# Half of one weight tile moved onto eight of the sixteen DMA engines, at the end of a decode block's weight stream

## The chip, the cores and the metric

The kernel runs on one core of a Trainium2 chip. The metric is device time in microseconds (us) of one launch. Before the change the median of three runs is 774.22 us (774.18 to 774.46).

## The reference

A decoder block for one token in each of two sequences (B = 2, D = 1024), all in float32: layer norm, cached attention with 32 query heads on 4 key/value heads of 128 over 32768 cached positions, and beside it a dense layer with SiLU; both are added to the input.

```python
xn = _layernorm(x, axis=-1)
return x + _A_ref(xn, A_k_cache, A_v_cache, A_wq, A_wo) + _B_ref(xn, B_w1, B_w2)

# _A_ref: q = x @ wq; softmax(q k^T / sqrt(Dh)) v, then  o.reshape(B, Sq, Hq * Dh) @ wo
# _B_ref: h = silu(x @ w1) with 3584 columns;  out = h @ w2
```

Keys, values and weights are some 331 MB, and each of them is used once.

## The kernel before, in words

SBUF holds three buffers `bufA`, `bufB` and `bufC` of 128 partitions x 16384 floats (8 MB each). Everything large passes through them, by transfers that one queue, SP's, issues in program order (`load`, L203). First come wq and w1 and their matmuls. Then eight loops, one for each pair of key/value head and sequence, take two blocks of keys and two of values, 8 MB each.

The last part is the product with the output weights, cut into 60 row tiles of 128 rows x 1024 columns: 32 of wo, 28 of w2. They add into one result. `plan` (L344) loads wo's first half into bufA, its second into bufC, and the first 16 tiles of w2 into bufB. When TensorE has finished with bufA (`i_wo0`, L376), the last 12 tiles of w2 go there in nine pieces (L377), each with a semaphore of its own (`piece4` to `piece12`): six tiles, two tiles, then three times one tile, then the last tile in four quarters. `stream` (L335) issues the pieces from the list of their cuts; `tiles` (L352) walks over the row tiles and lets TensorE wait for the piece that ends a tile. Row tile 57 is the third last (columns 9 D to 10 D of bufA, the tenth tile there). The quarters of row tile 59 have a loop of their own (L383). The result of tile 59 goes through ScalarE to `ot` (L389) and by a transfer of ScalarE's queue to the output (L390).

A source of 128 rows x n columns moves as 128 packets of n x 4 bytes, one for each partition, shared by 16 DMA engines: eight packets on each. Each engine works through the queue's transfers in their order, and a piece has landed when the last of its engines has signalled.

## Time and profile before

| | |
|---|---|
| median of three runs | 774.22 us |
| the profiled execution: its time | 774.62 us |
| the profiled execution: its span from first to last instruction | 773.1 us |
| TensorE busy with matmuls | 391.9 us, 51% |
| moved from memory | 331 MB, 429 GB/s over the span |
| DMA engines busy | 99.2% on SP's queue |

The profile divides the span into 40 slices and gives for each the busy share of every engine and of the 16 DMA engines. Rows of the trace give an instruction's start from the span's begin, the engine, the program line, and what ended the idle time ahead of it. A share of DMA of 1.00 is all 16 engines busy, 0.50 eight of them.

### The profile page before, as it was taken

What the parts mean: (1) busy time and instruction counts of PE and PEld (TensorE: products, weight loads), DVE (VectorE), ACT (ScalarE), POOL (GpSimd) and SP (SyncE); (2) the same over time, 40 slices, a digit from 0 to 9 for tenths busy, and PEclk for the clock granted to TensorE, in tenths of its full rate; (3) what the DMA queues carried; (4) which work ended last, traced back from release to release, by engine and by line L of the source; (5) the groups of instructions that cost most, each with busy time, mean ns of one, the idle gap of its engine ahead of it and who ended that gap; (6) DMA issues with size and microseconds to landing.
All of it is one profiled execution on the core that took longest, in us unless ns stands there. A gap on an engine that the chain in (4) does not pass through costs nothing. (4 is left out here: it accounts for less than half of the span.)

```text
span 773.1 us, 6135 instructions
## 1 busy us (share of the span) xinstructions
PE 391.9 (51%) x2736; PEld 121.8 (16%) x2736; DVE 130.5 (17%) x241; ACT 30.6 (4%) x49; POOL 3.0 (0%) x10
## 2 busy tenths in 40 slices
PE   1545645454545444545454555454554454555476
PEld 1111211111111111111111111111211121111111
DVE  2000015001410150015001410141014001410000
ACT  0000101000100010001000000000001000000000
POOL 1000000000000000000000000000000000000000
PEclk9977677677677677677677667667767667667679
DMA  9999999999999999999999999999999999999997
GB/s 384 434 435 431 434 435 434 435 434 434 434 434 434 434 434 434 434 434 434 434 434 434 431 434 434 431 434 434 434 434 434 434 434 434 434 434 434 420 427 302
DMA packets 7094, 331.51 MB, mean 429 GB/s; under 512 B 798, under 2 KB 1318, under 8 KB 1708
## 3 DMA queue, kind: packets, MB, share of 16 engines
q1 hardware_dynamic: 7056, 331.35, 99.2%
q8 instruction: 6, 0.10, 0.0%
q10 hardware_dynamic: 28, 0.02, 0.0%
q14 instruction: 4, 0.03, 0.0%
HBM read 331.37 MB, written 0.01 MB: 429 GB/s over the span
## 5 line engine op out<-in xcount | busy, mean ns | idle before, releaser
L97 PE MATMUL ps<-bufB,qT 128*32 128x512 f32 x512 | 73.8, 740 | 82.3 <-PEq L52 82.3
L97 PE MATMUL po<-bufB,st 128*32 128x512 f32 x512 | 72.3, 728 | 80.2 <-PEq L52 80.2
L97 PE MATMUL ps<-bufA,qT 128*32 128x512 f32 x512 | 72.9, 733 | 66.4 <-PEq L52 66.4
L97 PE MATMUL po<-bufA,st 128*32 128x512 f32 x512 | 74.6, 748 | 49.5 <-PEq L52 49.5
L250 DVE STREAM_TRANSPOSE st<-ps 128x512 f32<-128x512 f32 x32 | 22.9, 717 | 245.4 <-PE ps L97 245.4
L97 PEld LDWEIGHTS ps<-bufB,qT 128*32 128x32 f32 x512 | 20.2, 132 | 135.9 <-issue 135.9
L97 PEld LDWEIGHTS po<-bufB,st 128*32 128x32 f32 x512 | 19.9, 131 | 132.6 <-issue 132.6
L286 DVE RECIPROCAL rl<-smA 128x8 f32<-128x8 f32 x8 | 1.7, 208 | 222.7 <-PE smA L97 222.7
L97 PEld LDWEIGHTS ps<-bufA,qT 128*32 128x32 f32 x512 | 20.0, 131 | 112.7 <-issue 112.7
L97 PEld LDWEIGHTS po<-bufA,st 128*32 128x32 f32 x512 | 20.5, 134 | 97.1 <-issue 97.1
L252 DVE TENSOR_REDUCE mx<-st 128x8 f32<-128x512 f32 x32 | 34.8, 1086 | 1.1
L273 ACT ACTIVATE st<-st 128x512 f32<-128x512 f32 x32 | 20.2, 630 | 359.7 <-DVE st L272 358.7
L278 DVE TENSOR_REDUCE ls<-st 128x8 f32<-128x512 f32 x32 | 33.5, 1068 | 0.8
L97 PE MATMUL ps<-bufB,xnT 128*32 128x512 f32 x112 | 18.5, 737 | 14.6 <-PEq L52 14.6
L272 DVE TENSOR_TENSOR st<-st,gmax 128x512 f32<-128x512 f32 x32 | 21.2, 685 | 0.3
L97 PE MATMUL ps<-bufA,xnT 128*32 128x512 f32 x64 | 9.8, 778 | 13.1 <-PEq L52 13.1
L97 PE MATMUL ps<-bufC,oT 128*32 128x512 f32 x64 | 10.0, 790 | 9.9 <-DMA bufC<-in_wo 9.9
L97 PE MATMUL ps<-bufC,xnT 128*32 128x512 f32 x64 | 8.7, 705 | 10.7 <-DMA bufC<-in_w 10.7
L284 ACT COPY ob<-po 128x512 f32<-128x512 f32 x8 | 4.7, 585 | 232.8 <-PE po L97 232.8
L97 PE MATMUL ps<-bufA,oT 128*32 128x512 f32 x64 | 9.4, 750 | 8.6 <-DMA bufA<-in_wo 8.6
L97 PE MATMUL smA<-ident,rm 128*8 128x128 f32 x16 | 3.6, 314 | 18.6 <-PEq L52 18.6
L188 DVE COPY qall<-ps 128x16 f32<-128x16 f32 x4 | 0.5, 170 | 62.1 <-PE ps L97 62.1
(65 smaller groups left out, 109.3 us busy)
## 6 DMA issues: line engine op xcount, KB each, us to landing
bufB<-in_w SPq DMA_DIRECT2D x1, 6144.0 KB, 26.1
bufB<-in_w SPq DMA_DIRECT2D x1, 5632.0 KB, 43.0
bufA<-in_w SPq DMA_DIRECT2D x1, 3072.0 KB, 36.5
bufB<-in_w SPq DMA_DIRECT2D x1, 2560.0 KB, 48.7
bufA<-in_w SPq DMA_DIRECT2D x3, 512.0 KB, 40.3
bufA<-in_w SPq DMA_DIRECT2D x1, 1024.0 KB, 38.7
bufA<-in_w SPq DMA_DIRECT2D x4, 128.0 KB, 38.1
bufA<-in_kt SPq DMA_DIRECT2D x8, 29.2
```

Of the source, the lines that this page charges most:

```text
L97: return nc.tensor.matmul(o, lhsT, rhs, start=start, stop=stop)
L188: m = V.tensor_copy(qall[:, B * h:B * (h + 1), :].rearrange("p b (j i) -> p b j i", j=2), o[:, :, 2 * j:2 * j + 2, :].rearrange("p i j b - ...
L250: t = dve.mark(V.transpose(st[:, a].rearrange("p j m -> p (j m)"), ps[a]))
L252: m = dve.mark(V.tensor_reduce(mx[:, a, :], st[:, a].rearrange("p j (r m) -> p m (j r)", r=4), AX.X, ALU.max))
L272: act.wait(dve.mark(V.tensor_sub(e8, e8, gmax.to_broadcast([P, 64, REP]))))
L273: expd.append(act.mark(nc.scalar.activation(st[:, a], st[:, a], AF.Exp, scale=SCALE)))
L278: t = dve.mark(V.tensor_reduce(ls[:, a - 1, :], e8.rearrange("p n m -> p m n"), AX.X, ALU.add))
L284: act.tell(tob, act.mark(nc.scalar.copy(ob, po)))
L286: t = dve.mark(V.reciprocal(rl, smA[:, :REP]))
```

## The change

The list of cuts gets one more entry, so that row tile 57 comes in two transfers of half a tile's width (512 columns) each. The first half is an ordinary piece. The second half does not come from `w2` but from a new input `w2h`, which the host fills with the same numbers laid out as 16 x 8 x 512: element (r, e) is the row of partition 16 e + r. The transfer reads it with the axis e outermost, as 8 x 16 rows of 512 floats. TensorE waits for both halves ahead of tile 57, and the quarters' semaphores move on by one place.

```diff
-    pieces = []
+    pieces, w2h = [], w2h.rearrange("r e n -> e r n")
...
             s = sem(f"piece{len(pieces)}")
-            load(buf[:, lo:hi], src[:, lo:hi], s, *ticks)
+            if buf is bufA and src is not wo[0] and hi == 10 * D:
+                load(buf[:, lo:hi], w2h, s, *ticks)
+            else:
+                load(buf[:, lo:hi], src[:, lo:hi], s, *ticks)
...
-            pe.wait((next(s for hi, s in ends if hi >= (i + 1) * D), 16))
+            pe.wait(*((s, 16) for hi, s in ends if i * D < hi < (i + 1) * D),
+                    (next(s for hi, s in ends if hi >= (i + 1) * D), 16))
...
-    ends = [*stream(bufA, w2[:, W:], (0, 6 * D, 8 * D, 9 * D, 10 * D, lo, lo + QW, lo + 2 * QW, lo + 3 * QW,
+    ends = [*stream(bufA, w2[:, W:], (0, 6 * D, 8 * D, 9 * D, 9 * D + D // 2, 10 * D, lo, lo + QW, lo + 2 * QW, lo + 3 * QW,
                                       lo + D), i_wo0)]
...
-        pe.wait((ends[5 + u][1], 16))
+        pe.wait((ends[6 + u][1], 16))
...
+    half = arrays["w2"][:, (FT - 3) * D + D // 2:(FT - 2) * D]
+    arrays["w2h"] = lay(half, (8, 16, D // 2), (1, 0, 2), (16, 8, D // 2))
```

On SP's queue, at its end, where the pieces of w2 for bufA are issued (`in_w` is w2, `in_w2h` the new input):

```order
 L206 DMA bufA<-in_w 128x2048 [waits pe]
-L206 DMA bufA<-in_w 128x1024 [waits pe] x3
+L206 DMA bufA<-in_w 128x1024 [waits pe]
+L206 DMA bufA<-in_w 128x512 [waits pe]
+L206 DMA bufA<-in_w2h 128x1x512 [waits pe]
+L206 DMA bufA<-in_w 128x1024 [waits pe]
 L206 DMA bufA<-in_w 128x256 [waits pe] x4
```

The queue issues ten transfers there instead of nine; the four quarters stay last.

On TensorE, at row tiles 56 to 58 (`acc` is the result's bank; piece numbers count the transfers of this part):

```order
 L97 MATMUL acc<-bufA,hT 32x256 [waits piece6]
 L97 MATMUL acc<-bufA,hT 32x256 x3
-L97 MATMUL acc<-bufA,hT 32x256 [waits piece7]
+L97 MATMUL acc<-bufA,hT 32x256 [waits piece8,piece7]
 L97 MATMUL acc<-bufA,hT 32x256 x3
-L97 MATMUL acc<-ob,fold 32x256 [waits dve,piece8]
+L97 MATMUL acc<-ob,fold 32x256 [waits dve,piece9]
```

The matmuls and their order are the same; tile 57 waits for two semaphores instead of one.

## Rows read from the trace of the kernel before

**Rows 1.** The profile page: its slices and its DMA queues.
```profile
DMA  9999999999999999999999999999999999999997
GB/s 384 434 435 431 434 435 434 435 434 434 434 434 434 434 434 434 434 434 434 434 434 434 431 434 434 431 434 434 434 434 434 434 434 434 434 434 434 420 427 302
...
q1 hardware_dynamic: 7056, 331.35, 99.2%
q8 instruction: 6, 0.10, 0.0%
...
q14 instruction: 4, 0.03, 0.0%
```

**Rows 2.** The chain that ended last: start us, us, what.
```profile
728.16 0.43 SPq L206
...
728.64 5.67 SPq L206
...
734.35 11.63 SPq L206
745.98 0.04 issue
746.02 24.35 DMA bufA<-in_w
770.37 0.04 issue
770.41 0.36 PE acc L97 x8
...
770.80 0.37 ACT ot L389
```

**Rows 3.** Timeline of TensorE from 768 us: start, us, instruction, idle before.
```profile
767.64 0.82 PE L97 MATMUL acc<-bufA,hT 128*32 128x256 f32 x12
768.80 0.64 PE L97 MATMUL acc<-ob,fold 128*32 128x256 f32 x8 [0.34 <-DMA bufA<-in_w]
769.25 0.95 PE L97 MATMUL acc<-bufA,hT 128*32 128x256 f32 x32
770.41 0.32 PE L97 MATMUL acc<-bufA,hT 128*32 128x64 f32 x8 [0.21 <-DMA bufA<-in_w]
```

**Rows 4.** Stretches of 0.25 us; the last two columns are DMA share and GB/s.
```profile
767.25:767.50 0.25, 0.25 (x8) 0.07 (x4) 0.00 (x0) 0.00 (x0) 0.00 (x0) 1.00 1.00 352
767.50:767.75 0.25, 0.25 (x12) 0.15 (x8) 0.08 (x1) 0.00 (x0) 0.00 (x0) 1.00 0.69 234
767.75:768.00 0.25, 0.25 (x12) 0.13 (x8) 0.25 (x1) 0.00 (x0) 0.00 (x0) 1.00 0.55 193
768.00:768.25 0.25, 0.25 (x12) 0.00 (x0) 0.25 (x1) 0.00 (x0) 0.00 (x0) 1.00 0.52 184
768.25:768.50 0.25, 0.21 (x4) 0.00 (x0) 0.12 (x1) 0.00 (x0) 0.00 (x0) 1.00 0.53 184
768.50:768.75 0.25, 0.00 (x0) 0.00 (x0) 0.00 (x0) 0.00 (x0) 0.00 (x0) 1.00 0.43 148
768.75:769.00 0.25, 0.20 (x4) 0.16 (x8) 0.00 (x0) 0.00 (x0) 0.00 (x0) 1.00 0.31 107
769.00:769.25 0.25, 0.25 (x8) 0.13 (x4) 0.00 (x0) 0.00 (x0) 0.00 (x0) 1.00 0.14 49
769.25:769.50 0.25, 0.25 (x12) 0.16 (x8) 0.00 (x0) 0.00 (x0) 0.00 (x0) 1.00 0.07 25
```

**Rows 5.** DMA packets from 769.6 to 770 us: packets, MB, share of 16 engines.
```profile
q14 instruction: 1, 0.01, 6.5%
q1 hardware_dynamic: 1, 0.00, 0.1%
```

**Rows 6.** DMA packets from 753 to 754 us, instruction fetch.
```profile
q8 instruction: 1, 0.02, 6.9%
```

**Rows 7.** DMA packets from 764.6 to 765 us, those of 4 KB.
```profile
DMA packets 49, 0.16 MB, mean 410 GB/s; under 512 B 9, under 2 KB 9, under 8 KB 49
...
q1 hardware_dynamic: 49, 0.16, 103.3%
```

**Rows 8.** DMA packets from 7.5 to 7.75 us; q10 carries two of 2 KB.
```profile
q10 hardware_dynamic: 2, 0.00, 4.2%
```

## The prediction

> **What bounds the kernel now.** I read the page's slices first, then the chain that ended last, then the last four microseconds in detail. The slices say that the DMA engines are busy in 39 of 40 slices at about 434 GB/s and only the last slice falls, to 302 GB/s [rows 1]. So nearly all of the 774 us is the weights' and the cache's own bytes, and no byte is removed by this change: 256 KB are carried by other engines. What it can move is the end, when the sixteen engines run dry.

> The chain shows how that end is made: SP's last issue is out at 746.0, its transfer lands 24.35 us later at 770.37, four matmuls and their companions take 0.36 us, and ScalarE's copy 0.37 us [rows 2]. TensorE has its work done before: it stands idle for 0.34 us ahead of tile 58 and for 0.21 us ahead of the last quarter, both times for a transfer into bufA [rows 3]. So the landing of the last quarter sets the time, and a microsecond of its landing is a microsecond of the kernel.

> That landing is the latest of sixteen engines, and they are far from even. The reader is to see this in the share of DMA engines [rows 4]: 1.00 up to 767.5, about 0.54 from 767.75 to 768.5, 0.31 before 769.0, 0.14 before 769.25, 0.07 after it. A share of 0.54 is eight or nine engines: eight ran dry at about 767.6, the other eight run on, and one of them alone (0.07 x 16 = 1.1 engines) until about 769.6. After that there is one more instruction fetch of 6.5% x 16 x 0.4 = 0.42 us and a single packet of no size, the last signal [rows 5]. Call the engine that ends last L1, and the two that end shortly before it (0.14 x 16 = 2.2 engines until 769.25) L2 and L3.

> Why eight are late can be read as well. The program's instructions come by the same engines: six packets on one queue, four on another [rows 1]. One of the large ones took 6.9% x 16 x 1 us = 1.10 us [rows 6]. The late engines' surplus after 767.75 is the sum of shares x 16 x 0.25: 0.55 + 0.52 + 0.53 + 0.43 + 0.31 + 0.14 + 0.07 = 2.55, times 4 or 10 engine-us, 1.3 us for each of eight. So being late by about one fetch explains it, with L1 hit more than once. No view tells which engines were hit, by their numbers.

> **The change part by part.** *Packets.* A 4 KB packet takes at most 103.3% x 16 x 0.4 / 40 = 0.165 us (the nine small signals are counted in) [rows 7], so tile 57 costs each engine 8 x 0.165 = 1.32 us now. A packet of 2 KB took 4.2% x 16 x 0.25 / 2 = 0.084 us [rows 8]. The first half is eight such packets on each engine, 0.67 us. The second half has an outermost axis of eight; if it goes to eight engines, each of these gets sixteen packets, 1.34 us, and the others none. Together the eight need 2.02 us, **0.70 more** than now, and the other eight 0.67 us, **0.65 less**. Per engine-microsecond nothing is saved; the sum over all grows by 8 x 0.05 = 0.4 engine-us, 0.02 us of the core.

> *Which eight.* This decides the sign. If the eight were just those that run dry first, everybody would end between 768.3 and 769.0. The rows give no reason for that: the lateness comes from fetches, which as far as the trace shows have nothing to do with the numbers of the engines that a transfer with eight outer rows takes. I treat it as a draw of eight out of sixteen.

> [...]

> *The end, if L1 is among the eight* (1 in 2): its 0.70 us come on top, the fetch of 0.42 us stays in its way, and the landing moves from 770.37 to 771.07. *If L1 is not, but L2 or L3 is:* L1 ends its data at 769.6 - 0.65 = 768.95, ahead of the fetch at 769.6; L2 ends at about 769.15 + 0.70 = 769.85. From the end of L1's data to its landing are 770.37 - 769.6 = 0.77 us, of which 0.42 are the fetch, so 0.35 us stay: the landing is at 770.2, 0.2 us earlier than now. That none of the three is among the eight has a chance of 8/16 x 7/15 x 6/14 = 0.10 (all three among the other eight).

> *The waits and SP's queue.* Tile 57 waits for two signals instead of one. Both precede the quarters that set the end, and TensorE's idle 0.34 and 0.21 us [rows 3] cover the instruction; without that cover I would put it between 0 and 0.04 us, the gap between two steps of the chain [rows 2]. On SP one more transfer is issued, for 0.43 us [rows 2]. SP waits there for room: the eighth issue took 5.67 us, the ninth 11.63 us, until 746.0. So the tenth waits for the next transfer to drain. At one piece later that is about 754; if room is counted in packets, sixteen for the new half, it is some 5 us later still. The quarters begin to move at about 766, so at least 7 us are left over, and nothing is queued behind them on SP. I take zero. The new host layout costs nothing on the device, as the bytes are the same.

> *The sum.* The profiled execution is 774.62 us for a span of 773.1, 0.40 above the median of 774.22; all terms are differences, and I put them on the median. With one of L1 to L3 among the eight, the ends are 774.22 - 0.2 = 774.0 and 774.22 + 0.70 = 774.9. Between these I take the middle, **774.5 us**, as L1 itself is in half of the draws. A measurement of this kernel tells 0.2%, 1.55 us, from no change; neither end reaches that.

> **The rivals.** *The early engines get the work.* None of L1 to L3 is among the eight. If the later ones of the other late engines are, they end at about 768.9 + 0.70 = 769.6, landing at 769.95, which is 0.4 us less than now: 773.8. If all late ones are outside, L1 sets the end with data at 768.95 and its landing at 769.3, 1.1 us less: 773.1. For it: it is the one placement in which the change evens out the ends [rows 4]. Against it: one in ten draws. Even this best case stays under the 1.55 us, since no engine can lose more than its 0.65 us and the one fetch.

> *The second half runs slower than its packets' price, on the slower side.* Eight engines read every eighth row of a new array and write sixteen neighbouring partitions each, beside the eight others; the trace has no transfer of this form. The fetch of 16 KB, an unusual one too, took 1.10 us [rows 6] where 16 KB in four 4 KB packets take 0.66 [rows 7], a factor of 1.67. With it the sixteen packets take 2.24 us, 0.9 more, and a late engine among the eight ends 1.6 us later: 775.8. It decides from 0.137 us for a packet on (0.084 + 0.85 / 16). Against it: bytes per engine are alike in all rows, 25 GB/s for 4 KB and 24 for 2 KB.

> *The transfer is spread over all sixteen after all.* Then each engine has sixteen packets of 2 KB for tile 57, 16 x 0.084 = 1.34 against 1.32 us, and the time is 774.2. For it: the destination still has 128 partitions outermost.

> **How the numbers follow.** The forecast (one of the three latest is among the eight) gets 0.78, the early engines 0.10, the slow half 0.06, the spread over sixteen 0.06. The range takes the forecast's ends of 774.0 and 774.9, 0.3 us to either side for what runs differ by (774.18 to 774.46) and for fetches that fall on other engines, and on the low side part of the early case: 773.5 to 775.2. Faster by over 0.2% would need 1.55 us, which no case gives: 0.01. Slower by over 0.2% is the slow half: 0.06. The rest, 0.93, is no change.

> **What the profile of the changed kernel would show.** Right: between 766 and 769 us the share of DMA falls in another shape, half the packets in the second half's time being on eight engines; a tail in which one engine works alone until about 770.3, or several until 769.9; SP's last issue after 750, its landing still last in the chain; the same idle places of TensorE. Wrong: a tail that falls steeply from 1.00 near 768.5 (the early engines took the work), a share near 0.5 for two microseconds or more ahead of the quarters (the half is slow), or SP's last issue beyond 766 (its queue bounds). A time under 772.7 or over 775.8 would mean that a cause outside the last four microseconds moved.

## The result and the profile after

The changed kernel takes **776.94 us** in the median of seven runs (776.79 to 777.3), against 774.22 of the kernel before beside it (seven runs): a ratio of 1.0033 with an interval of 1.0024 to 1.0042. It is **2.7 us slower**. The forecast was 774.5 with a range up to 775.2, "no change".

The profiled execution has 776.91 us and a span of 775.4. On its page the busy times are as before; what stands out are the last two slices of the rate, 415 and 251 GB/s, which were 427 and 302 [rows 1].

```profile
span 775.4 us, 6137 instructions
...
GB/s 383 439 440 437 439 437 433 440 430 433 436 433 433 433 433 433 433 433 433 433 433 433 433 433 433 433 433 433 433 433 433 433 433 433 433 433 433 435 415 251
...
q1 hardware_dynamic: 7192, 331.35, 99.2%
```

SP's queue carries 136 packets more than before (7192 for 7056). 128 of them are the extra transfer's data and eight are small ones, by the page's packets under 512 B (806 for 798); a transfer of all sixteen engines has sixteen small ones, as 7056 = 49 x (128 + 16) for the 49 before. That fits eight engines; no row names them.

The chain that ended last of the changed kernel (start us, us, what) answers to [rows 2]:

```profile
745.83 0.04 issue
745.87 6.03 SPq L206
751.90 0.04 issue
...
752.42 20.24 DMA bufA<-in_w
772.66 0.04 issue
772.71 0.36 PE acc L97 x8
...
773.09 0.37 ACT ot L395
```

SP's ninth issue starts at 751.95, the tenth, that of the last quarter, at 752.42. The tenth takes SP 9.99 us, until 762.41, which is still 3.4 us ahead of the first packet of a quarter (765.84). The end is still the landing of the last quarter, four matmuls and the copy, but the landing is at 772.66 instead of 770.37. The two profiled executions differ by 776.91 - 774.62 = 2.29 us, and all of it lies in that landing; the rest of the 2.7 is that the profiled execution before is 0.40 us above its median.

TensorE's timeline of the changed kernel, the answer to [rows 3]:

```profile
768.61 0.60 PE L97 MATMUL acc<-bufA,hT 128*32 128x256 f32 x8
770.13 0.64 PE L97 MATMUL acc<-bufA,hT 128*32 128x256 f32 x8 [0.92 <-DMA bufA<-in_w2h]
771.07 0.64 PE L97 MATMUL acc<-ob,fold 128*32 128x256 f32 x8 [0.30 <-DMA bufA<-in_w]
...
772.71 0.32 PE L97 MATMUL acc<-bufA,hT 128*32 128x64 f32 x8 [0.23 <-DMA bufA<-in_w]
```

There is a new idle place of 0.92 us, ahead of tile 57, for the eight-engine transfer; the two old ones, 0.30 and 0.23 us, are nearly as before (0.34 and 0.21). The stretches show why it is late. Stretches of the changed kernel, whose last two columns are the DMA share and GB/s:

```profile
763.00:764.00 1.00, 1.00 (x8) 0.20 (x4) 0.00 (x0) 0.00 (x0) 0.00 (x0) 0.50 1.01 401
764.00:765.00 1.00, 1.00 (x12) 0.31 (x8) 0.00 (x0) 0.00 (x0) 0.00 (x0) 0.50 1.07 313
765.00:766.00 1.00, 1.00 (x12) 0.28 (x8) 0.00 (x0) 0.00 (x0) 0.00 (x0) 0.50 0.99 212
766.00:767.00 1.00, 1.00 (x8) 0.20 (x4) 0.00 (x0) 0.00 (x0) 0.00 (x0) 0.50 1.11 225
767.00:768.00 1.00, 1.00 (x8) 0.20 (x4) 0.00 (x0) 0.00 (x0) 0.00 (x0) 0.50 1.02 272
...
771.00:772.00 1.00, 0.93 (x20) 0.58 (x24) 0.00 (x0) 0.00 (x0) 0.00 (x0) 1.00 0.11 38
```

The same of the kernel before:

```profile
764.00:765.00 1.00, 1.00 (x8) 0.20 (x4) 0.00 (x0) 0.00 (x0) 0.00 (x0) 0.50 1.03 410
765.00:766.00 1.00, 1.00 (x12) 0.32 (x8) 0.00 (x0) 0.00 (x0) 0.00 (x0) 0.75 1.01 403
766.00:767.00 1.00, 1.00 (x14) 0.24 (x10) 0.00 (x0) 0.00 (x0) 0.00 (x0) 1.00 1.05 387
```

The share stays near 1.0 and the rate falls to half. All sixteen engines are busy, with packets that take twice their time. From 764 to 767 the loss is (410 + 403 + 387) - (313 + 212 + 225) = 450 KB, 1.1 us at 400 GB/s, and from 767 to 768 the rate is still 272 GB/s at a share of 1.02. The packets say it too. Half a microsecond of the changed kernel, from 766 us:

```profile
DMA packets 61, 0.12 MB, mean 238 GB/s; under 512 B 6, under 2 KB 20, under 8 KB 61
...
q1 hardware_dynamic: 61, 0.12, 113.6%
```

Half a microsecond of the kernel before, from 765 us:

```profile
DMA packets 53, 0.20 MB, mean 401 GB/s; under 512 B 4, under 2 KB 4, under 8 KB 53
...
q1 hardware_dynamic: 53, 0.20, 100.3%
```

Before, 0.20 MB took 8.0 engine-us, 40 us for a MB; now 0.12 MB take 9.1, 76 us for a MB. The size of the packets is not the reason: between 764.5 and 767 us the changed kernel's packets of 4 KB took 0.28 to 0.31 us on average, where 0.163 stood before, and those of 2 KB 0.14 to 0.17, where its own took 0.084 to 0.093 ahead of 764.

### The profile page after: what moved, and what is told of

Its sections match the earlier page's. It is cut to its first block, busy times and chain, and to the rows that moved or that the text cites. A ratio compares the mean times of both kernels' runs of the same rounds, so it can differ in the third digit from the quotient of the medians.

```text
span 775.4 us, 6137 instructions
## 1 busy us (share of the span) xinstructions
PE 392.0 (51%) x2736; PEld 121.4 (16%) x2736; DVE 130.4 (17%) x241; ACT 30.6 (4%) x49; POOL 3.0 (0%) x10
## 3 DMA queue, kind: packets, MB, share of 16 engines
q1 hardware_dynamic: 7192, 331.35, 99.2%
## 5 line engine op out<-in xcount | busy, mean ns | idle before, releaser
L97 PE MATMUL ps<-bufB,hT 128*32 128x512 f32 x64 | 9.8, 779 | 3.7 <-DMA bufB<-in_w 3.7
```

The lines of the kernel that those rows point to most:

```text
L97: return nc.tensor.matmul(o, lhsT, rhs, start=start, stop=stop)
```

## The experiments

Three causes were open: the smaller packets and the extra transfer (SMALL), the way in which eight engines read the new array (READ), and the way in which they write sixteen neighbouring partitions each (WRITE). Beside them stood the forecast's own term, load on a late engine.

### Both halves as ordinary pieces

```diff
-                load(buf[:, lo:hi], w2h, s, *ticks)
+                load(buf[:, lo:hi], src[:, lo:hi], s, *ticks)
```

> Both halves of row tile 57 come as ordinary pieces out of w2, on all engines; the extra transfer, the 2 KB packets and the second wait stay. If 2 KB packets or the extra transfer cost the time (theory SMALL), it stays at 776.5 to 777.2. If it is the eight-engine transfer, by its reads (theory READ), by its writes (theory WRITE) or by its load on late engines, it is 774.0 to 774.5, like before, and the data rate stays near 400 GB/s in the last ten microseconds.

Measured: 774.61 us against 774.65 of the kernel before on that chip, ratio 1.0001 (0.9992 to 1.0011); its rate from 765 to 766 us is 393 GB/s. SMALL falls: 2 KB packets, one more transfer and the second wait cost nothing that can be measured.

### The source laid out by engine

```diff
-    pieces, w2h = [], w2h.rearrange("r e n -> e r n")
+    pieces, w2h = [], w2h[:, :16, :]
...
-    arrays["w2h"] = lay(half, (8, 16, D // 2), (1, 0, 2), (16, 8, D // 2))
+    arrays["w2h"] = np.pad(np.asarray(half).reshape(8, 16, D // 2), ((0, 0), (0, 1), (0, 0)))
```

> The eight-engine transfer as in the change, but its source is laid out so that each engine reads sixteen consecutive rows (32 KB) instead of every eighth row. Destination, engines and packets are the same. READ (the rows that eight engines fetch lie in one another's way in memory): the packets return to about 0.085 us and the time to 774.9, the load on the late engines alone. WRITE (eight engines that write sixteen neighbouring partitions each get in one another's and the others' way): 776.6 to 777.2, with the rate near 215 to 275 GB/s between 764.5 and 768.5 as in the change.

Measured: 776.71 us against 774.65, ratio 1.0027 (1.0016 to 1.0038), 230 GB/s from 765 to 766. Each engine now reads 32 KB in one run (the array has a spare row between the engines' runs), and nothing is gained that the intervals could show. READ in this form falls. The next pair keeps the reads and varies the writes.

### The same reads, written to chosen partitions

Two transfers of eight partitions each, step 4 and step 16, into columns of bufA that are free by then; two more with step 4 begin at partition 32 and at partition 64. These kernels leave out the second half of row tile 57. Both transfers signal one semaphore, and tile 57 waits for 32 in place of 16; below, with four transfers, for 64. The cut for step 4 from partition 0:

```diff
-                load(buf[:, lo:hi], w2h, s, *ticks)
+                for q in range(2):
+                    load(bufA[q:q + 7 * 4 + 1:4, 12 * D:].rearrange("p (r n) -> p r n", r=8),
+                         w2h[:, 8 * q:8 * q + 8, :], s, *ticks)
...
```

> Leaves out the second half of row tile 57: the eight engines read the same source and carry the same 256 KB in 2 KB packets, but write them to unused columns of bufA, in two transfers over the partitions 0, 4, ..., 28 and 1, 5, ..., 29 (engine e always on partition 4 e or 4 e + 1). READ: no change of the time, 776.5 to 777.2. WRITE: the contention is gone, the rate holds near 400 GB/s up to 767, and 774.6 to 775.0 stays, the 0.7 us of load on a late engine.

> As the run with partitions 0, 4, ..., 28, also without the second half of row tile 57, but on the partitions 0, 16, ..., 112 and 1, 17, ..., 113. READ: the same time as that run. WRITE: slower than that run by 1 us or more (775.7 to 777.5), since the partitions are those whose sharing the change has. If both runs are fast and alike, neither the source nor the places but the sixteen neighbouring partitions in turn matter.

> The same on 64, 68, ..., 92 and 65, 69, ..., 93, the partitions that the other eight engines serve in ordinary transfers (without the second half of row tile 57). OWN: every one of the eight shares a way with one busy engine, packets of both take about twice as long for some 1.3 us: a dip to 200 to 250 GB/s, the time 0.7 to 1.6 us above the run on 0, 4, ..., 28. If sharing among the eight alone were the cause, no dip and the same time as that run.

Measured:

| partitions of the eight engines | time, us | before beside it | ratio, interval | GB/s, 765 to 766 |
|---|---|---|---|---|
| 0, 4, ..., 28 | 774.94 | 774.65 | 1.0005 (0.9995 to 1.0015) | 387 |
| 32, 36, ..., 60 | 775.09 | 774.68 | 1.0004 (0.9994 to 1.0013) | 391 |
| 64, 68, ..., 92 | 777.78 | 774.68 | 1.0043 (1.0029 to 1.0058) | 207 |
| 0, 16, ..., 112 | 778.45 | 774.65 | 1.0051 (1.0034 to 1.0067) | 207 |

Stretches of the run on 32, 36, ..., 60:

```profile
764.00:765.00 1.00, 1.00 (x12) 0.32 (x8) 0.00 (x0) 0.00 (x0) 0.00 (x0) 0.50 1.03 397
765.00:766.00 1.00, 1.00 (x12) 0.20 (x8) 0.00 (x0) 0.00 (x0) 0.00 (x0) 0.77 1.04 391
766.00:767.00 1.00, 1.00 (x16) 0.35 (x12) 0.00 (x0) 0.00 (x0) 0.00 (x0) 1.00 1.03 378
...
770.00:771.00 1.00, 0.80 (x36) 0.55 (x32) 0.00 (x0) 0.00 (x0) 0.00 (x0) 1.00 0.03 12
```

Stretches of the run on 64, 68, ..., 92:

```profile
764.00:765.00 1.00, 1.00 (x12) 0.20 (x4) 0.00 (x0) 0.00 (x0) 0.00 (x0) 0.50 1.11 317
765.00:766.00 1.00, 1.00 (x8) 0.20 (x4) 0.00 (x0) 0.00 (x0) 0.00 (x0) 0.50 1.02 207
766.00:767.00 1.00, 1.00 (x8) 0.20 (x4) 0.00 (x0) 0.00 (x0) 0.00 (x0) 0.50 1.06 224
767.00:768.00 1.00, 1.00 (x12) 0.24 (x8) 0.00 (x0) 0.00 (x0) 0.00 (x0) 0.90 1.09 242
```

Engines, source, bytes, packets and number of transfers are the same in both; a shift of the destination by 32 partitions halves the rate and costs 2.7 us. So the partitions written decide here. In this pattern the eight engines' writes to 0 to 31 and to 32 to 63 left the rate at 387 and 391 GB/s, those to 64 to 95 at 207. WRITE holds, and the rates are those that OWN expected. The trace names no engine and no partition of a packet, so which engine an ordinary transfer uses for a partition is OWN's supposition, which the rates bear out, also where an expectation puts it as given. Two runs are dearer than was expected: the one from 64 (3.1 us above before, 2.8 above the run on 0, 4, ..., where 0.7 to 1.6 stood) and the one on 0, 16, ... (778.45 where 775.7 to 777.5 stood). A later run bears on this.

The clean runs also show the forecast's own term. One engine alone still moves quarters after 770 us (12 GB/s in the last row above), which before ended at about 769.6 [rows 4]. Their last packet ends at 770.20 in the run from 32 and at 770.27 in the one from 0, where it was 769.64 before: 0.56 and 0.63 us later, near the forecast's 0.70. So the engine that ends last is very probably one of the eight. The last landing of the run from 32 is at 770.89, 0.52 later than before; in time the two clean runs are 0.3 and 0.4 us above theirs, inside the intervals.

### Four blocks of 32 partitions

```diff
-                load(buf[:, lo:hi], w2h, s, *ticks)
+                for q in range(4):
+                    load(buf[32 * q:32 * q + 32, lo:hi], w2h[:, 4 * q:4 * q + 4, :], s, *ticks)
...
-    arrays["w2h"] = lay(half, (8, 16, D // 2), (1, 0, 2), (16, 8, D // 2))
+    arrays["w2h"] = lay(half, (4, 8, 4, D // 2), (0, 2, 1, 3), (16, 8, D // 2))
```

> The complete result, the second half of row tile 57 by eight engines, sixteen 2 KB packets each, as in the change; but cut into four transfers of 32 partitions, in which engine e writes the partitions 4 e to 4 e + 3 of each block. The eight are never on partitions 16 apart at once. SPACING (it is the 16 partitions between the eight engines' places that makes them share a way into SBUF): the contention goes, and the load on a late engine stays, 774.6 to 775.2. FOREIGN (any write to partitions that another engine serves in ordinary transfers costs): half of the blocks, those of partitions 64 to 127, still cost, 775.5 to 776.3.

Measured: 776.3 us against 774.64, ratio 1.0021 (1.0012 to 1.003). SPACING falls, FOREIGN holds. Stretches of this run:

```profile
764.00:764.50 0.50, 0.50 (x8) 0.21 (x4) 0.00 (x0) 0.00 (x0) 0.00 (x0) 0.50 1.04 402
764.50:765.00 0.50, 0.50 (x4) 0.00 (x0) 0.00 (x0) 0.00 (x0) 0.00 (x0) 0.50 1.05 397
765.00:765.50 0.50, 0.50 (x8) 0.21 (x4) 0.00 (x0) 0.00 (x0) 0.00 (x0) 0.50 1.13 266
765.50:766.00 0.50, 0.50 (x8) 0.06 (x4) 0.00 (x0) 0.00 (x0) 0.00 (x0) 0.50 0.98 203
```

The rate holds until 765, where the run from 64 had fallen to 317 GB/s between 764 and 765, and then it halves. The delay is about that of two blocks, eight packets of 0.084 us on each engine; it fits that the blocks on partitions 0 to 63 go at the full rate and the third does not.

### Twice as much, earlier, and on sixteen engines

The whole row tile 57 by eight engines:

```diff
-    ends = [*stream(bufA, w2[:, W:], (0, 6 * D, 8 * D, 9 * D, 9 * D + D // 2, 10 * D, lo, lo + QW, lo + 2 * QW, lo + 3 * QW,
+    ends = [*stream(bufA, w2[:, W:], (0, 6 * D, 8 * D, 9 * D, 10 * D, lo, lo + QW, lo + 2 * QW, lo + 3 * QW,
...
-    arrays["w2h"] = lay(half, (8, 16, D // 2), (1, 0, 2), (16, 8, D // 2))
+    arrays["w2h"] = lay(half, (8, 16, D), (1, 0, 2), (16, 8, D))
```

> All of row tile 57 (512 KB) by one eight-engine transfer as the change has it, 16 packets of 4 KB on each engine. If bytes written in this manner set the price, both terms double: contention of about 2 us to 4, load from 0.7 to 1.3 us, together 779 to 780.5. If the price is one for the transfer (a start, a switch), it stays at 777 to 778.

Measured: two runs, 779.81 and 783.3 us, ratio 1.009 (1.0068 to 1.0113); the profiled one is the lower, and its rate lies at 197 to 221 GB/s from 764 to 771. The time is not to be read closely, as its last 48 matmuls took 2.83 us, many at a granted clock of 0.50. The landing of row tile 58 is clearer: 768.8 us before, 771.0 in the change, 773.1 here, so twice the bytes cost about twice as much. The price goes with the bytes; a price for the transfer as such does not show.

The half transfer in the first piece, for row tile 48:

```diff
...
-    ends = [*stream(bufA, w2[:, W:], (0, 6 * D, 8 * D, 9 * D, 9 * D + D // 2, 10 * D, lo, lo + QW, lo + 2 * QW, lo + 3 * QW,
+    ends = [*stream(bufA, w2[:, W:], (0, D // 2, D, 6 * D, 8 * D, 9 * D, 10 * D, lo, lo + QW, lo + 2 * QW, lo + 3 * QW,
...
```

> The eight-engine half transfer is that of row tile 48, the first piece of this part, some 8 us ahead of its place in the change; tile 57 comes whole. If what is lost is the engines' time wherever it falls, the time stays at 776.4 to 777.2. If only the end of the stream suffers (the early transfers have slack), it is 774.2 to 774.9.

Measured: 776.75 us against 774.64, ratio 1.003 (1.0019 to 1.0041). The rate dips to 242 GB/s from 755 to 756 and is back at 393 from 764 to 765. At this place, too, the loss is the same.

All sixteen engines, eight rows each:

```diff
-    arrays["w2h"] = lay(half, (8, 16, D // 2), (1, 0, 2), (16, 8, D // 2))
+    arrays["w2h"] = lay(half, (16, 8, D // 2), (1, 0, 2), (8, 16, D // 2))
```

> The second half again from the extra array, but with an outermost axis of 16 rows groups of eight, so that all sixteen engines take eight packets each; no load is moved. If the sixteen then write eight neighbouring partitions each, they are 8 partitions apart and SPACING expects some sharing, 774.9 to 776.0 and a dip of the rate near 765; if they keep the partitions of an ordinary transfer, 774.0 to 774.7 and no dip.

Measured: 775.72 us against 774.64, ratio 1.0015 (1.0005 to 1.0024), with 268 to 276 GB/s from 765 to 768. By its layout this transfer moves no load, and the dip is there all the same, where the ordinary halves kept 386 to 393 GB/s from 765 to 767. So this transfer, with sixteen outermost in its source, did not go like an ordinary row transfer; that each engine gets eight neighbours fits, but was not looked at by itself, and is not shown.

### Two engines only

These kernels, too, leave out the second half of row tile 57; two engines carry 128 KB in its place.

```diff
-                for q in range(2):
-                    load(bufA[q:q + 7 * 4 + 1:4, 12 * D:].rearrange("p (r n) -> p r n", r=8),
-                         w2h[:, 8 * q:8 * q + 8, :], s, *ticks)
+                for q in range(4):
+                    load(bufA[64 + q:64 + q + 5:4, 12 * D:].rearrange("p (r n) -> p r n", r=8),
+                         w2h[2 * q:2 * q + 2, :8, :], s, *ticks)
...
```

(with `q:q + 5:4` in place of `64 + q:64 + q + 5:4` for the run on partitions 0 to 7)

> Leaves out the second half of row tile 57; instead two engines carry 128 KB, 32 packets of 2 KB each, to unused columns of partitions 0 to 7 (four transfers with two outer rows, partitions q and 4 + q), their own by the theory OWN. No dip: all packets keep 0.16 us for 4 KB, 0.084 us for 2 KB. The two end 32 x 0.084 - 0.65 = 2.0 us later, so the time is between 774.0 (early engines) and 776.3 (if the latest engine is one of them).

> The same on partitions 64 to 71, which two of the other eight engines serve. DIRECT (only engines that share a way lose time): four engines run at half rate, the other twelve keep 0.16 us for 4 KB, the rate falls by a quarter at most, to some 320 GB/s. CLOG (one shared way holds up all sixteen): 4 KB packets take 0.25 us or more on all engines, the rate falls towards 200 GB/s for as long as the two write there, five us, and the time is 2 us or more above that of the run on partitions 0 to 7.

Measured: 775.14 us on partitions 0 to 7 (ratio 1.0004, 0.9994 to 1.0014) and 777.23 on 64 to 71 (1.0032, 1.002 to 1.0045), before beside them 774.67. Stretches of the run on 0 to 7:

```profile
765.00:766.00 1.00, 1.00 (x12) 0.23 (x8) 0.00 (x0) 0.00 (x0) 0.00 (x0) 0.71 1.02 382
766.00:767.00 1.00, 1.00 (x16) 0.27 (x12) 0.00 (x0) 0.00 (x0) 0.00 (x0) 1.00 1.01 360
```

Stretches of the run on 64 to 71:

```profile
765.00:766.00 1.00, 1.00 (x12) 0.24 (x8) 0.00 (x0) 0.00 (x0) 0.00 (x0) 1.00 1.11 302
766.00:767.00 1.00, 1.00 (x16) 0.33 (x12) 0.00 (x0) 0.00 (x0) 0.00 (x0) 1.00 1.08 197
767.00:768.00 1.00, 0.52 (x12) 0.03 (x4) 0.69 (x1) 0.00 (x0) 0.00 (x0) 1.00 1.04 187
...
769.00:770.00 1.00, 0.00 (x0) 0.00 (x0) 0.00 (x0) 0.00 (x0) 0.00 (x0) 1.00 0.61 175
```

CLOG holds. Two engines that write where two others write bring all sixteen to half the rate, 187 to 197 GB/s, with the share of busy time still at 1.0. The two others alone could have cost a quarter. The packets show it one by one: each of 4 KB that began between 765.5 and 768.5 us took 0.28 us or more, on whichever engine, and none took over 0.173 in the run on 0 to 7. From 766.5 to 767.5 us 0.194 MB took 17.0 engine-us, 87 us for a MB; in the run on 0 to 7, from 765.0 to 765.4, 0.153 MB took 6.3, 41 us for a MB. This fits the dear run from 64 above: every packet in flight pays, not only those that share.

The hold on the others ends before the writes do. The two engines' 2 KB packets still took 0.12 to 0.16 us until 769.70, but from 769.25 on most packets of the quarters took 0.046 to 0.06 us, as in the kernel before; in the last row above a share of 0.61 moves 175 GB/s, where 1.04 moved 187. By then many engines have run dry. So the hold on all goes with many engines at work; whether it needs them was not tested.

(The time of the profiled execution on 64 to 71 is not to be read closely: its last 48 matmuls took 2.8 us, most of it at a granted clock of 0.50, and are part of its end.)

## Why the prediction was wrong

**What bounds the kernel** was right. The end is the landing of the last quarter, before and after; TensorE's work hides in the idle places; SP's queue and the second wait cost nothing (the run with ordinary halves shows the last two, at a ratio of 1.0001). On SP's queue the zero came out right on a wrong reading: the issues of 5.67 and 11.63 us are the seventh and the eighth of the nine, not the eighth and the ninth, and the changed kernel's tenth was out at 762.41, not at 754 or five us later; 3.4 us were left over, not 7. What an issue of that length waits for no row names; room in the queue was the forecast's own reading.

**The step that failed** is the price of the second half's packets: "A packet of 2 KB took ... 0.084 us [rows 8]", and with it "sixteen packets, 1.34 us". That row is of two packets of another, tiny transfer near the launch. As a price of ordinary halves it holds (ratio 1.0001). The change's packets go to sixteen neighbouring partitions for each engine, and there 2 KB took 0.14 to 0.17 us, and a MB 76 engine-us instead of 40, on all sixteen engines, ordinary packets included. The forecast counted packets for each engine and took the engines to be independent of one another; the runs with two engines show that they aren't (from 766 to 767 us 197 GB/s with the two on 64 to 71, 360 with them on 0 to 7).

**The rival** "The second half runs slower than its packets' price" named the place, and a threshold of 0.137 us for a packet, which the 0.14 to 0.17 us measured are above, but gave it 0.06. Its price of 1.6 us was too low: it slowed only the sixteen packets, by a factor of 1.67, and left the others alone. The argument against it ("bytes per engine are alike in all rows") compared only transfers of one form of writing, so it could not speak to another. Where a sentence says that the trace has no transfer of this form, 0.06 is too little for what it may cost.

**Which eight** was a draw in the forecast, and L1 is very probably among them, as the lone engine after 770 us in the clean runs says. Its 0.70 us measured some 0.3 to 0.4 us in time, with intervals of about 0.8 us to either side, 0.52 in the landing of one run, and 0.56 and 0.63 in the end of its data. So of the 2.7 us some 0.3 to 0.6 are the forecast's load and the rest the writes; the split rests on runs on several chips and is an estimate. With that, the early engines' rival is out for this placement.

**Why eight are late** was called explained by the fetches. The trace before has nine of them ahead of the stream's last microseconds, six of 16 KB at 0.91 to 1.10 us and three of 8 KB at 0.32, some 7.1 us in all; the forecast's own sum of the lateness is 10.2 engine-us. So these fetches alone fall short of it, and the rest is open.

**The sign to watch** was chosen badly. I looked for a slow half in the share of busy engines ("a share near 0.5"). A 4 KB packet that took 0.28 to 0.31 us in place of 0.163 counts as busy for all of it; the share stayed at 0.99 to 1.11 from 764 to 768, and the GB/s column beside it showed the loss, 212 to 313. A time over 775.8 was to mean a cause outside the last four microseconds; the loss does begin earlier, between 764 and 765.

**Left open.** Why the writes of two engines hold up engines that write elsewhere. The trace gives a packet's time, not what it waits for. A rival to the sharing itself is untested, too: in each slow run on chosen partitions some of the eight engines write to partitions 64 to 127, and no run has them write only partitions of one another, below 64. That any such write is slow, and not only one to a partition where another engine writes, is not excluded.

## What to carry to other kernels

Before a transfer is given to fewer engines, or cut by an outermost axis of the source, ask which partitions each engine will then write: here a row transfer over all 128 partitions kept 387 to 410 GB/s from 764 to 767 us, and each of the forms tried in which, by OWN, an engine wrote partitions of another's ordinary share took the rate down to between 187 and 276 GB/s while most engines were at work. To even out the ends of the engines is worth some 1.2 us here at most (an estimate: 10.2 engine-us over sixteen engines end at about 768.4, in place of 769.6 [rows 4]), and so is easily spent; none of the versions run was faster than the kernel before. In a stretch where the DMA engines bound, read bytes per second and time per packet, not the busy share: from 765 to 766 us a share of 1.01 went with 403 GB/s before, and 0.99 with 212 in the change.

## What the runs showed of the hardware

It matters which partitions an engine writes: eight engines on 4 e and 4 e + 1, and on the same plus 32, leave ordinary transfers beside them at full rate (387 and 391 GB/s), and on the same plus 64 bring all down to 207 GB/s. That fits OWN, partitions which are an engine's own in an ordinary row transfer; the trace does not name them.

Two engines are enough to slow all sixteen: with the two on partitions 64 to 71 the rate was 197 and 187 GB/s from 766 to 768 us at a share of 1.08 and 1.04, and with them on 0 to 7 it was 360 from 766 to 767 at 1.01.

Instruction fetches are in the same count of sixteen engines as the data: from 753 to 754 us a packet of 16 KB took 1.10 us of one engine [rows 6], 6.9%, and SP's queue had 92.8%. At the end of the stream half of the engines were 1.3 us behind the others on average, an estimate from [rows 4]; how much of that is the fetches is not shown.
